# Interleaving an MLP group with the last attention tiles: own buffer, searched queue order, lighter VectorE work and LayerNorm sums on GpSimd

## The chip, the cores and the metric

The kernel runs on 1 core of one Trainium2 chip. The metric is device time in microseconds (us), the median of several executions. The span in a profile is a little shorter than the device time (228.3 against about 230 us), because it runs from the first to the last instruction. Every execution is classed as fast or slow by its length and its granted TensorE clock; only fast ones are compared.

## The reference

One transformer-like block over x of shape 1x2048x448 in bf16, cut to what matters:

```python
h  = x + A(layernorm(x), wqkv, wo)          # attention
out = h + B(layernorm(h), w1, w2, w3, w4)   # token-shift MLP

# A: 16 heads of 28; query s sees keys s, s-2, ..., s-14 (8 keys, dilation 2)
#    softmax over these 8, weighted sum of v, then @ wo
# B: g  = gelu(layernorm(z) @ w1)                    448 -> 448
#    gs = four quarters of g, shifted by +1, -1, +2, -2 tokens
#    x1 = z + gs @ w2                                448 -> 448
#    y  = x1 + gelu(layernorm(x1) @ w3) @ w4         448 -> 1792 -> 448
```

The 2048 tokens are handled as 4 attention tiles of 512 and 4 MLP groups of 512. Because of the token shifts the MLP groups are not the attention tiles: group 0 takes 128-row blocks from tiles 0 and 1.

## The kernel before

The kernel is a program that writes a program. It lists every operation with its reads and writes, then a scheduler gives each engine one fixed queue. The engines then run their queues in order, so a blocked operation blocks what stands behind it on its engine. The parts that matter here, with cuts marked:

```python
h3T = [arv(o, 128, NF * 512).rearrange("p (f n) -> p f n", f=NF) for o in (0, R_WQ)]
# both GELU buffers of the MLP lie in an arena: number 0 over wqkv and its padded copy,
# number 1 over the attention's output scratch (of, ob)

def ln_stats(kind, src, i):                                   # VectorE, one 128-row block
    dve("bn_stats", D + 20, out=st6[:, kind, i, :], in_=src)
    dve("bn_aggr", 64, out=mv[:, kind, i, :], in_=st6[:, kind, i, :])

def inv_std(slot, kind, i0, n, s1=1.0, s2=EPS):               # GpSimd, 4 operations for 4 blocks
    pool("tensor_scalar", ..., out=vtmp, in0=mv[..., 1], scalar1=s1, scalar2=s2, ...)
    S.add("pool", "tensor_tensor", ..., out=rstd, in0=vtmp, in1=mhalf, op=ALU.pow)
    pool("tensor_scalar", ..., out=nmr, in0=mv[..., 0], scalar1=-1.0, ...)
    pool("tensor_tensor", ..., out=nmr, in0=nmr, in1=rstd, op=ALU.mult)
# normalize(): one block, on VectorE or ScalarE, whichever the scheduler finds free ("flex")
# (cut)
            # end of two head groups of an attention tile: O is [128, 2, 512] in PSUM
            dve("transpose", 1024, psum=True, out=of[:, os_, :, :], in_=O(lambda p: p[:, :, :]))
            o4 = of[:, os_, :, :].rearrange("p u (b d) -> p (u b) d", d=32)
            dve("reciprocal", 160, out=rz[:, os_, :], in_=o4[:, :, 28])
            dve("scalar_tensor_tensor", 1024, out=ob[...], in0=rz[...broadcast...], scalar=UP, in1=o4, ...)
            dve("transpose", 1024, out=oT[:, par, c - 1:c + 1, :], in_=ob[:, os_, :, :])   # 16 bit
# (cut) the end of the order in which the phases are listed:
    phase_att(2); phase_WO(1); phase_QK(3); phase_V(3); phase_att(3); phase_WO(2)
    phase_B1(0); phase_B1(1); phase_B2(0); phase_WO(3); phase_B1(2); phase_B1(3)
    phase_W3(0); phase_B2(1); ...          # W3 and B3 are the two big matmuls of an MLP group
```

The scheduler is greedy: of the operations that are ready it takes the first that can start, ties broken by a list of 137 phase names. The phases are: A1 the first LayerNorm; QK, V the projections; att, av the attention; WO the output projection with its residual add; B1 a LayerNorm, w1 and GELU; B2 the shifted w2, the add and the statistics of the next LayerNorm; W3 that LayerNorm, w3 and GELU; B3 w4 and the output.

## Time and profile before

| | before |
|---|---|
| device time, median (range) of 4 runs beside the changed kernel | 229.96 us (229.75 to 231.16) |
| profiled span, mean granted TensorE clock | 228.3 us, 0.964 |
| busy: TensorE, VectorE, ScalarE, GpSimd | 205.6, 133.8, 118.4, 57.4 us |
| first projection, last matmul | 12.16, 222.70 us |

The page of the profile. Digits are the busy share of 40 equal slices in tenths; PE is TensorE, DVE VectorE, POOL GpSimd; PEclk is the granted clock.

```profile
span 228.3 us, 3663 instructions
...
PE   7799899989999859996389999999999999999990
...
DVE  7597778979979997989988308941001243101221
...
PEclk9999999999999976999959999999999999999997
...
PE 61%; DVE 23%; POOL 6%; ACT 4%; DMA 2%; issue 2%; POOLq 0%
```

The second half is TensorE without a break. In the first half VectorE is the fuller engine, TensorE has two deep holes (the slices with 5 and 3), and after each its clock drops (to 0.57 and 0.51 in the stretches of 6 us below). The last line is the share of each engine in the chain of waits, the path that ended last.

The same in a table of stretches (busy time and number of instructions of each engine, then granted clock, DMA share and GB/s). The first two lines are the two stages, split where the unbroken run of TensorE begins; the others are a hole and two stretches behind holes.

```profile
core 0: us, PE busy (x) PEld busy (x) DVE busy (x) ACT busy (x) POOL busy (x), PEclk, DMA share, GB/s
12.16:115.77 103.61, 89.25 (x971) 47.55 (x970) 91.44 (x147) 77.61 (x91) 28.25 (x52) 0.95 0.38 82
115.77:222.70 106.93, 106.93 (x519) 51.47 (x519) 33.72 (x71) 36.24 (x38) 20.43 (x32) 0.98 0.16 37
...
78.00:84.00 6.00, 2.67 (x82) 1.85 (x82) 5.90 (x10) 6.00 (x9) 0.85 (x2) 0.86 0.51 90
84.00:90.00 6.00, 5.83 (x32) 3.32 (x33) 4.11 (x9) 4.85 (x7) 3.80 (x7) 0.57 0.36 68
...
114.00:120.00 6.00, 5.16 (x14) 1.91 (x15) 5.00 (x6) 0.04 (x1) 0.00 (x0) 0.51 0.10 19
```

The chain of waits at the seam (start, length, what, number of instructions):

```profile
110.78 1.14 DVE arena L1206
...
112.33 2.11 DVE arena L1206
...
114.47 1.26 DVE oT L1206
...
115.77 106.94 PE ps L1206 x519
```

Stage 1 ends in VectorE's work on the last attention tile: a transpose out of PSUM, the softmax division, and the 16-bit transpose `oT` that the last output projections wait for. The first W3 matmul of MLP group 0 follows only at 120.45 us (this is what "first matmul of group 0" means in all that follows; the group's w1 and w2 matmuls run before it in both kernels), behind 14 output projections that take 4.85 us, most of them at half clock (0.51 from 114 to 120 us).

Some groups of instructions (shapes, count, total busy us, mean ns of one, idle before):

```profile
L1206 DVE STREAM_TRANSPOSE oT<-arena 128x1024 bf16<-128x1024 bf16 x8 | 10.0, 1245 | 0.3
...
L1206 DVE TENSOR_SCALAR lntm<-xin,mv,rstd 128x448 bf16<-128x448 bf16 x13 | 4.8, 400 | 2.7 <-POOL nmr L1206 2.6
```

### The profile page before, as it was taken

The page shows a single profiled execution, that of the slowest core. Times are in us where ns is not written, and L with a number is a line of the kernel's source. Part 1 is how long each engine was busy: PE and PEld are TensorE (multiplying, and loading weights), DVE is VectorE, ACT ScalarE, POOL GpSimd, SP SyncE. Part 2 cuts the span into 40 slices and gives each one's busy share as a digit, 9 for nine tenths or more (in the row PEclk, how much of TensorE's full clock was granted, in tenths as well). Part 3 has the DMA queues.
Part 4 walks back from the last instruction along what each step waited for, and adds up shares of the span by engine and source line. Part 5 has one row for each costly group of instructions (what it writes and reads, how often), then busy time and mean ns, then how long its engine had stood idle before and what let it go on. Part 6 is the DMA issues. An engine that isn't in the chain of part 4 may idle for free.

```text
span 228.3 us, 3663 instructions
## 1 busy us (share of the span) xinstructions
PE 205.6 (90%) x1529; PEld 103.0 (45%) x1529; DVE 133.8 (59%) x244; ACT 118.4 (52%) x134; POOL 57.4 (25%) x107
## 2 busy tenths in 40 slices
PE   7799899989999859996389999999999999999990
PEld 2346355345445534553234455554444445444540
DVE  7597778979979997989988308941001243101221
ACT  2537776774979879748903750423651152154100
POOL 8631611000241044053702300883000008000000
PEclk9999999999999976999959999999999999999997
DMA  5924682469300054004400400146000103300110
GB/s 154 295 84 87 82 195 38 92 183 290 97 4 0 3 92 92 3 0 92 81 15 0 86 6 3 36 97 132 3 0 20 40 3 64 88 0 20 46 43 26
DMA packets 32462, 15.36 MB, mean 67 GB/s; under 512 B 23416, under 2 KB 31992, under 8 KB 32440
## 3 DMA queue, kind: packets, MB, share of 16 engines
q1 hardware_dynamic: 32440, 15.06, 28.8%
q8 instruction: 14, 0.23, 0.5%
q14 instruction: 8, 0.07, 0.1%
HBM read 7.45 MB, written 1.84 MB: 41 GB/s over the span
## 4 chain that ended last, share of the span: by engine, by line
PE 61%; DVE 23%; POOL 6%; ACT 4%; DMA 2%; issue 2%; POOLq 0%
PE ps L1206 61%; DVE arena L1206 6%; DVE st L1206 5%; DVE pt L1206 3%; POOL rstd L1206 3%; DVE oT L1206 3%; DMA hT<-lntm 2%; DVE xin L1206 2%; ACT pt L1206 2%; DVE mv L1206 1%; ACT qk L1206 1%; POOL nmr L1206 1%; DVE xb L1206 1%; POOL msk L1206 1%; DVE rz L1206 1%
## 5 line engine op out<-in xcount | busy, mean ns | idle before, releaser
L1206 PE MATMUL ps<-actT,w_s 112*128 112x512 bf16 (+1 forms) x288 | 68.0, 389 | 0.4 <-DMA actT<-lntm 0.4
L1206 DVE TENSOR_TENSOR xb<-ps,xb 128x448 bf16<-128x448 f32 (+1 forms) x24 | 18.4, 772 | 66.2 <-PE ps L1206 66.2
L1206 ACT ACTIVATE arena<-ps 128x1024 bf16<-128x1024 f32 x28 | 28.6, 1023 | 50.6 <-PE ps L1206 50.5
L1206 PEld LDWEIGHTS ps<-actT,w_s 112*128 112x128 bf16 (+1 forms) x288 | 30.7, 108 | 33.0 <-issue 1.9
L1206 PE MATMUL ps<-w_s,arena 128*128 128x448 bf16 x224 | 44.4, 353 | 0.0
L1206 ACT ACTIVATE pt<-ps 110x1024 bf16<-110x1024 f32 x32 | 31.0, 1022 | 5.9 <-PE ps L1206 5.9
L1206 PEld LDWEIGHTS ps<-w_s,arena 128*128 128x128 bf16 x224 | 21.8, 98 | 21.1 <-ACT arena L1206 0.2
L1206 PE MATMUL ps<-hT,arena 112*128 112x512 bf16 x128 | 28.8, 380 | 1.9 <-DMA hT<-lntm 1.0
L1206 POOL TENSOR_SCALAR vtmp<-mv 128x4 f32<-128x4 f32 (+1 forms) x17 | 3.3, 193 | 93.6 <-DVE mv L1206 92.9
L1206 DVE TENSOR_TENSOR pt<-pt,msk 110x1024 bf16<-110x1024 bf16 x32 | 20.4, 682 | 1.1 <-ACT pt L1206 1.1
L1206 PE MATMUL ps<-wo_s,oT 128*128 128x448 bf16 x64 | 15.8, 399 | 4.5 <-ACT gT L1206 3.5
L1206 PEld LDWEIGHTS ps<-hT,arena 112*128 112x128 bf16 x128 | 12.0, 97 | 17.1 <-ACT pt L1206 1.8
L1206 DVE BATCH_NORM_STATS2 st<-xin 128x6 f32<-128x448 bf16 x32 | 19.2, 601 | 0.2
L1206 POOL TENSOR_TENSOR rstd<-vtmp,mhalf 128x4 f32<-128x4 f32 (+1 forms) x17 | 17.8, 1049 | 1.4
L1206 ACT ACTIVATE lntm<-xin,nmr,rstd 128x448 bf16<-128x448 bf16 x19 | 13.5, 755 | 8.6 <-POOL nmr L1206 8.6
L1206 POOL TENSOR_TENSOR xb<-xb,xin 128x448 bf16<-128x448 bf16 x16 | 16.7, 1072 | 2.4 <-DVE lntm L1206 1.5
L1206 ACT ACTIVATE qk<-ps 128x1024 bf16<-128x1024 f32 x12 | 12.3, 1024 | 6.8 <-PE ps L1206 6.7
L1206 PE MATMUL ps<-arena,hT 112*110 112x448 bf16 x64 | 15.0, 360 | 0.3 <-ACT pt L1206 0.3
L1206 PE MATMUL ps<-qk 28*110 28x103 bf16 (+1 forms) x320 | 10.6, 226 | 4.7 <-ACT vt L1206 2.2
L1206 PE MATMUL ps<-w_s,gT 112*128 112x448 bf16 x64 | 13.1, 353 | 1.6 <-DVE xb L1206 1.6
L1206 PEld LDWEIGHTS ps<-wo_s,oT 128*128 128x128 bf16 x64 | 6.5, 107 | 13.2 <-ACT gT L1206 3.9
L1206 PEld LDWEIGHTS ps<-qk 28*110 28x110 bf16 x320 | 7.7, 132 | 10.0 <-ACT pt L1206 2.7
(58 smaller groups left out, 183.6 us busy)
## 6 DMA issues: line engine op xcount, KB each, us to landing
w_s<-in_B_w_dram SPq DMA_DIRECT2D x2, 1568.0 KB, 10.5
out_dram<-xb SPq DMA_DIRECT2D x16, 112.0 KB, 1.7
xin<-in_A_x_dram SPq DMA_DIRECT2D x3, 448.0 KB, 7.9
arena<-in_A_wqkv_dram SPq DMA_DIRECT2D x3, 392.0 KB, 5.4
w_s<-in_B_w_dram SPq DMA_DIRECT2D x2, 392.0 KB, 4.7
xin<-in_A_x_dram SPq DMA_DIRECT2D x4, 112.0 KB, 2.1
wo_s<-in_A_wo_dram SPq DMA_DIRECT2D x4, 98.0 KB
actT<-lntm SPq DMA_TRANSPOSE x8, 4.3
```

Of the source, the lines that this page charges most:

```text
L1206: inst = getattr(eng, op.meth)(**op.kw)
```

## The change

Its intent: let MLP group 0 run in TensorE's holes between the later attention tiles, for which its GELU output needs a buffer that does not lie over wqkv; take work off VectorE; and fix the place of each single operation in its queue by a search done beforehand. Five parts:

1. **Own buffer and phase order.** `h3T` of group 0 is its own tensor; the phases B1, B2 and W3 of group 0 are listed before the last attention tiles.
2. **Order.** The greedy scheduler with its phase names goes. A list of 674 numbers gives the priority of the items, a string of digits the engine of each flexible operation. Where the scheduler's own time model sees a gap on TensorE of over 0.35 us, it inserts dummy matmuls (256 columns of zeros) to hold the clock.
3. **LayerNorm sums.** `bn_aggr` leaves VectorE (44 of 48); seven small GpSimd operations per LayerNorm group compute mean and variance from the raw statistics.
4. **Paired softmax transposes.** The scaled output is written with pairs of 16-bit values interleaved, so the second transpose moves 512 32-bit elements instead of 1024 16-bit ones. Output projection slices then have stride 2.
5. **Start.** The masks are made after the first LayerNorm on GpSimd; transposes and evictions of the first tile go in half-size pairs.

The diff, cut to its core:

```diff
-    h3T = [arv(o, 128, NF * 512)... for o in (0, R_WQ)]
+    of = sb("of", [128, 2, 2, 512], F32)
+    ob = sb("ob", [128, 2, 4, 4, 32, 2], BF16)
+    h3T = [sb("h3T", [128, NF, 512], BF16), arv(0, 128, NF * 512)...]
 (cut: scheduler)
+        rank = [-1] * m
+        for r, w in enumerate(self.plan[0] if self.plan else range(m)):
+            rank[w] = r
+            if e == "pe" and self.filler and st > 13000.0 and st - free[e] > self.GAP:
+                ... # dummy matmuls up to the modelled start of the next one
 (cut)
     def ln_stats(kind, src, i):
         dve("bn_stats", D + 20, out=st6[:, kind, i, :], in_=src)
-        dve("bn_aggr", 64, out=mv[:, kind, i, :], in_=st6[:, kind, i, :])
+    def moments(kind, i0, n):
+        pool("tensor_tensor", 90, out=a, in0=st[:, :, 1], in1=st[:, :, 4], op=ALU.subtract)
+        pool("tensor_tensor", 90, out=a, in0=a, in1=a, op=ALU.mult)
+        pool("tensor_tensor", 90, out=b, in0=st[:, :, 2], in1=st[:, :, 5], op=ALU.add)
+        pool("tensor_scalar", 90, out=b, in0=b, scalar1=4.0 / D, scalar2=None, op0=ALU.mult)
+        pool("tensor_tensor", 90, out=a, in0=a, in1=b, op=ALU.add)
+    def sums(kind, i0, n):
+        pool("tensor_tensor", 90, out=m, in0=st[:, :, 1], in1=st[:, :, 4], op=ALU.add)
+        pool("tensor_scalar", 90, out=m, in0=m, scalar1=-0.5, scalar2=None, op0=ALU.mult)
 (cut)
-                dve("scalar_tensor_tensor", 1024, out=ob[...], in0=rz[...], scalar=UP, in1=o4, ...)
-                dve("transpose", 1024, out=oT[:, par, c - 1:c + 1, :], in_=ob[:, os_, :, :])
+                dve("tensor_tensor", 1110, out=ob[...].rearrange("p g k d e -> p g e k d"), in0=o4,
+                    in1=rz4.unsqueeze(4).broadcast_to([128, 4, 2, 4, 32]), op=ALU.mult)
+                dve("transpose", 580, out=oT[:, par, c - 1:c + 1, :].bitcast(F32),
+                    in_=ob[...].rearrange("p g k d e -> p (g k d e)").bitcast(F32))
 (cut)
+    phase_B1(0); phase_B1(1)
     phase_QK(3); phase_V(3)
+    phase_att(2)
+    phase_B2(0); phase_W3(0)
     phase_att(3); phase_WO(2)
+    phase_B1(2); phase_B3(0); phase_WO(3); phase_B1(3); ...
```

## The prediction

> **What bounds the kernel now.** Two stages with different limits. In the chain of waits, 115.8 to 222.7 us is one unbroken run of TensorE (519 matmuls, 106.9 us) at full clock: one matmul per 0.216 us at 512 columns, 0.189 at 448 (timeline). Before that the chain runs mostly through VectorE: in a table of 6 us stretches it is busy 102.7 of the first 120 us. There TensorE loses time: from 12 to 120 us it is idle 13 us, most of it at 78-84 (3.3), 102-108 (2.1) and 108-114 us (3.4). After two of these holes its granted clock falls to 0.57 and 0.51; 15 projection matmuls then run 0.43 us apart, 12 output projections 0.37. That costs some 5 us more. The first real projection starts at 12.0 us; after the last matmul come 5.5 us.
>
> [...]
>
> **What the change does.**
> 1. MLP group 0 (56 matmuls of 512 and 56 of 448 columns: 12.1 + 10.6 = 22.7 us of TensorE) can run between attention tiles 2 and 3. TensorE's work doesn't shrink; its holes get filled and the clock kept.
> 2. VectorE sheds 44 of 48 aggregates (180 ns each: 7.9 us) and half of each of 8 output transposes (1.25 us for 1024 elements of 2 or 4 bytes alike, so 512 four-byte elements about 0.65: 4.8 us): 13 us of 134, some 10 of it in the first stage, whose limit it is.
> 3. GpSimd gains seven small operations per LayerNorm group, 0.19 to 0.26 us each: 15 to 20 us in total (57 now), and 1.0 to 1.5 us more latency from statistics to normalisation; hidden where other work is queued.
> 4. Start: masks behind the first LayerNorm on GpSimd, no bias needed there, transposes and evictions in half-size pairs (0.69 us becomes about 0.4). First projection at about 10 us.
> 5. Searched order of single operations, and dummy matmuls in modelled gaps, free where the gap is real. Exponentials and GELU interleave more: a table load is 1.28 us on ScalarE (4 now; I expect 5 to 8).
>
> **Sum.** At most 2 (start) + 13 (holes) + 5 (clock) = 20 us can go, a floor near 210. I expect 2 + 8.5 + 4.5 = 15, and 1 to 2 lost to misjudged waits in a fixed order: about 216 us.
>
> Predicted: 216 us, 8 in 10 within 209 to 222. Faster by over 2%: 0.93; within 2%: 0.05; slower: 0.02.
>
> **What would show each step.** (1) TensorE idle between its first projection and last matmul under 6 us, mean clock above 0.98 (now 0.964), GELUs of group 0 before the last exponentials. (2) VectorE 117 to 124 us busy, output transposes 0.6 to 0.75 us. (3) GpSimd 70 to 80 us busy. (4) First projection at 9.5 to 10.5 us. (5) Dummies visible; TensorE's share 94% or more. The chain over 75% TensorE (now 61%).
>
> **What would make it wrong.** The queues are in order: if GpSimd's longer LayerNorm or table loads come later than the order's model assumes, TensorE stands before a matmul although others could run: 222 or more. Misplaced dummies delay real matmuls. If nearly every hole is filled and the tail shrinks too: 207 to 210.

The sum is at most 2 (start) + 13 (holes) + 5 (clock) = 20 us, of which 2 + 8.5 + 4.5 = 15 were expected, less 1 to 2: about 216 us. The 5 us of the clock were counted from the slow matmuls in the trace of before; that filling the holes would win them back was the author's estimate.

## More of the kernel before

Stage 1 has 103.61 - 89.25 = 14.36 us of TensorE idle; stage 2 has none. VectorE is busy for 91.44 of 103.61 us (88%) of stage 1.

## The result, and the profile after

| | before | after |
|---|---|---|
| device time, median (range) of 4 runs | 229.96 us (229.75 to 231.16) | 220.56 us (220.08 to 220.81) |
| ratio, 95% interval | | 0.9578 (0.9542 to 0.9615) |
| profiled span, granted clock | 228.3 us, 0.964 | 218.2 us, 1.000 |
| busy: TensorE, VectorE, ScalarE, GpSimd | 205.6, 133.8, 118.4, 57.4 us | 204.0, 127.5, 114.8, 73.0 us |
| first projection, last matmul | 12.16, 222.70 us | 11.33, 213.36 us |
| first matmul of MLP group 0 | 120.45 us | 107.31 us |

A ratio is the mean time of one kernel's fast runs over the mean of the other's fast runs of the same rounds on the same chip, so it is not quite the ratio of the medians quoted beside it.

The page after:

```profile
span 218.2 us, 3795 instructions
...
PE   5899999898999878999899999999999999999991
...
...
PEclk9999999999999999999999999999999999999999
...
PE 61%; DVE 12%; POOL 9%; ACT 8%; DMA 5%; issue 2%; SPq 1%
```

The clock no longer drops and no slice of TensorE is below 7 after the start. It looks as though the holes were filled. The chain of waits does not agree: TensorE's share is 61% as before, and VectorE's share went to GpSimd, ScalarE and DMA.

The stages, split where the first matmul of group 0 starts:

```profile
core 0: us, PE busy (x) PEld busy (x) DVE busy (x) ACT busy (x) POOL busy (x), PEclk, DMA share, GB/s
11.33:107.31 95.98, 89.89 (x1029) 50.25 (x1029) 84.49 (x122) 70.28 (x80) 36.72 (x80) 1.00 0.38 87
107.31:213.36 106.05, 105.78 (x521) 51.59 (x521) 34.24 (x61) 39.75 (x44) 30.59 (x70) 1.00 0.18 40
```

And of these, the dummies alone (the tile of zeros; here the columns are TensorE, weight load and VectorE):

```profile
11.33:107.31 95.98, 7.47 (x61) 5.77 (x60) 0.00 (x0) 1.00 0.38 87
```

This is the reading on which the rest of the document stands. Stage 1 of the changed kernel holds 1029 matmuls, of which 61 are of zeros (60 dummies and the last of those at the start): 968 real ones. The two tables of stages are cut at different events: the one of before at the unbroken run, which starts with 14 output projections. Cut at the first matmul of group 0 like the one of after, it reads:

```profile
12.16:120.45 108.29, 93.93 (x985) 49.52 (x984) 94.71 (x150) 77.61 (x91) 28.25 (x52) 0.94 0.36 78
120.45:222.70 102.25, 102.25 (x506) 49.50 (x504) 30.45 (x67) 36.24 (x38) 20.43 (x32) 1.00 0.17 38
```

So before the first matmul of group 0 there stood 985 matmuls (one of them of the start's, on zeros), and after the change 968. No W3 matmul of MLP group 0 moved into stage 1; on the contrary, 16 w1 matmuls moved out of it (48 of 64 ran before that event, now 32; the new list of phases has B1(3) only after B3(0)). The holes of stage 1 are 95.98 - 89.89 = 6.09 us of idle plus 7.47 us of dummies, 13.56 us together, against 14.36 us before. They were not filled with work of group 0; over half of them were painted over. Group 0's first matmul comes 120.45 - 107.31 = 13.1 us earlier, 0.8 of it because stage 1 starts earlier. What follows it got longer, from 102.25 to 106.05 us, with the 16 matmuls more, so 3.8 us are given back; after the last matmul 0.8 us are gained (228.3 - 222.70 = 5.6, and 218.2 - 213.36 = 4.8). That makes the 10.1 us of the span.

Why group 0 starts only at 107.31 us is in the chain of waits after (start, length, what; pieces called "issue", of 0.1 us at most, are left out without a mark):

```profile
72.28 1.01 DVE xin L1264
73.31 1.16 DVE st L1264 x2
74.55 2.38 POOL mom L1264 x5
...
80.56 4.53 DMA actT<-lntm
85.14 3.67 PE ps L1264 x16
...
90.52 1.28 ACT L1264
91.82 1.94 ACT pt L1264 x2
...
94.43 1.10 DVE xb L1264
...
96.79 1.19 POOL mom L1264 x2
...
100.94 0.40 DVE lntm L1264
...
104.45 2.82 PE ps L1264 x14
107.31 28.47 PE ps L1264 x137
```

Read it as a sequence: the residual of attention tile 1 (`xin`) at 72.28; its LayerNorm (`st` on VectorE, `mom` on GpSimd); a DMA transpose; the w1 matmuls; GELU, an activation table load, two exponentials that stood in the queue in between; the residual `xb` of the token-shift matmul; the next LayerNorm; and another DMA transpose, issued at 103.03 and 4.2 us long, while the last output projections run. (At its very end the chain goes by those projections: from 101.33 us through the division and the transposes of the last attention tile on VectorE. The DMA transpose lands at about 103.03 + 4.2 = 107.2 us, so the two paths end together.) That is 107.31 - 72.28 = 35.0 us from the moment group 0's tokens leave attention until its first matmul, and TensorE carries the chain for 3.67 + 2.82 = 6.5 us of it. By 107 us the attention is over (the last exponentials start at 91.82), so there is nothing left to interleave with.

The groups that answer to those of before:

```profile
L1264 DVE TENSOR_SCALAR lntm<-xin,rstd,nmr 128x448 bf16<-128x448 bf16 x16 | 7.1, 487 | 5.8 <-POOL nmr L1264 5.8
L1264 DVE STREAM_TRANSPOSE oT<-ob 128x512 f32<-128x512 f32 x8 | 5.6, 706 | 0.2
```

The output transposes fell by 4.4 us, and the aggregates by 7.8 us (from 48 at 180 ns, 8.5 us, to 4, 0.7 us), as costed. VectorE fell only by 6.3 us in total, because it now does 33 block normalisations instead of 25, and each takes 487 to 741 ns by group where it took 394 to 400: together 16.4 us instead of 9.0.

### The profile page after: what moved, and what is told of

Read it like the earlier page. It is cut to its first block, busy times and chain, and to the rows that moved or that the text cites. A ratio compares the mean times of both kernels' runs of the same rounds, so it can differ in the third digit from the quotient of the medians.

```text
span 218.2 us, 3795 instructions
## 1 busy us (share of the span) xinstructions
PE 204.0 (94%) x1587; PEld 105.4 (48%) x1587; DVE 127.5 (58%) x206; ACT 114.8 (53%) x130; POOL 73.0 (33%) x165
## 4 chain that ended last, share of the span: by engine, by line
PE 61%; DVE 12%; POOL 9%; ACT 8%; DMA 5%; issue 2%; SPq 1%
PE ps L1264 61%; POOL mom L1264 5%; DMA xin<-in_A_x_dram 3%; DVE st L1264 3%; POOL rstd L1264 3%; DVE lntm L1264 2%; DVE xb L1264 2%; ACT pt L1264 2%; DMA actT<-lntm 2%; ACT lntm L1264 2%; SPq L1264 1%; ACT qk L1264 1%; DVE pt L1264 1%; DVE ob L1264 1%; ACT xb L1264 1%
## 5 line engine op out<-in xcount | busy, mean ns | idle before, releaser
L1264 PE MATMUL ps<-actT,w_s 112*128 112x512 bf16 (+1 forms) x288 | 63.9, 380 | 1.9 <-ACT pt L1264 1.2
L1264 POOL TENSOR_TENSOR mom<-st 128x4 f32<-128x4 f32 x33 | 8.9, 287 | 56.8 <-DVE st L1264 56.8
L1264 ACT ACTIVATE arena<-ps 128x1024 bf16<-128x1024 f32 x14 | 14.1, 1019 | 20.2 <-PE ps L1264 20.2
L1264 ACT ACTIVATE h3T<-ps 128x1024 bf16<-128x1024 f32 x14 | 14.3, 1022 | 15.5 <-PE ps L1264 15.5
L1264 PE MATMUL ps<-w_s,h3T 128*128 128x448 bf16 x112 | 22.3, 353 | 0.0
L1264 PE MATMUL ps<-w_s,arena 128*128 128x448 bf16 x112 | 22.0, 353 | 0.0
L1264 PE MATMUL ps<-zz 128*128 128x256 bf16 (+1 forms) x82 | 14.8, 334 | 2.3 <-DVE zz L1264 2.3
L1264 ACT ACTIVATE lntm<-xb,nmr,rstd 128x448 bf16<-128x448 bf16 x8 | 5.5, 750 | 21.8 <-POOL nmr L1264 21.8
L1264 PEld LDWEIGHTS ps<-w_s,arena 128*128 128x128 bf16 x112 | 10.9, 98 | 10.4
L1264 PEld LDWEIGHTS ps<-w_s,h3T 128*128 128x128 bf16 x112 | 10.9, 98 | 10.4
L1264 PE MATMUL ps<-wo_s,oT 128*128 128x448 bf16 x64 | 13.5, 354 | 1.2 <-DVE oT L1264 0.7
L1264 ACT ACTIVATE qk<-ps 128x1024 bf16<-128x1024 f32 x12 | 12.2, 1024 | 4.4 <-PE ps L1264 4.4
```

The costliest lines, as they stand in the source:

```text
L1264: inst = getattr(eng, op.meth)(**op.kw)
```

## The experiments

Two readings compete at the start. One is the prediction's: TensorE is the resource, and the gain is its holes (filled by work, or by dummies for the clock). The rival is that TensorE does not limit stage 1 at all: a chain of waits through VectorE, ScalarE, GpSimd and DMA does, and the gain is that this chain became shorter, through lighter operations or through a better order. The text before each run names theories in its own words. Every result below was correct against the reference within its tolerance. The kernel before ran beside each set on the same chip, but the sets ran on different chips.

| run | set | median (range), us | ratio to before, 95% interval | first matmul of group 0, us |
|---|---|---|---|---|
| the change | | 220.56 (220.08 to 220.81) | 0.9578 (0.9542 to 0.9615) | 107.31 |
| no_fill | 1 | 220.27 (219.67 to 221.25) | 0.9565 (0.9509 to 0.9620) | 107.31 |
| swap_h3 | 1 | 220.84 (219.84 to 221.28) | 0.9596 (0.9549 to 0.9642) | 107.15 |
| mask_late | 1 | 220.42 (219.85 to 221.00) | 0.9567 (0.9517 to 0.9618) | 106.98 |
| t16 | 1 | 221.18 (220.76 to 221.69) | 0.9604 (0.9556 to 0.9653) | 107.58 |
| before_fill | 2 | 228.85 (227.13 to 229.64) | 0.9904 (0.9827 to 0.9981) | 118.45 |
| aggr_dve | 2 | 239.34 (237.55 to 242.63) | 1.0327 (1.0239 to 1.0415) | 113.24 |
| old_ops | 2 | 239.65 (236.04 to 240.69) | none given: two of four runs slow | 113.92 |
| new_ops | 2 | 254.03 (253.54 to 254.73) | 1.0994 (1.0931 to 1.1058) | 134.0 |
| new_search | 3 | 218.71 (217.63 to 221.92) | 0.9484 (0.9431 to 0.9538) | 104.44 |
| aggr_search | 3 | 219.44 (217.36 to 219.56) | 0.9476 (0.9432 to 0.9520) | 106.53 |
| old_search | 3 | 223.48 (221.45 to 224.51) | 0.9677 (0.9627 to 0.9727) | 107.14 |
| early_group0 | 4 | 212.82 (211.30 to 215.13) | 0.9200 (0.9146 to 0.9255) | 85.25 |

Before's medians of the sets: set 1 230.49, set 2 231.06, set 3 231.33, set 4 230.75 us. Medians and ranges include the slow runs (one each of aggr_dve, new_search and early_group0, two of old_ops); the ratios don't. One of the 11 executions of before in set 3 took 523.41 us and is left out of the ratios too.

### First set: one part undone, order kept

**no_fill: the dummies away.**

```diff
-    S.filler = lambda b: dict(out=ps[:, b, 0:256], lhsT=zz[:, 0:128], rhs=zz[:, 0:256], start=True, stop=True)
```

> The changed kernel with its 60 modelled filler matmuls left out, the order of everything else unchanged. Theory (dummies keep the clock, and are free because they stand in real holes): TensorE pauses of several us appear at 93-99 us and 102-104 us, the granted clock drops to about 0.5 after them, the first matmuls of group 0 run 0.43 us apart, and the time rises by 2 to 4 us to about 223. Rival (dummies stand in the way of real matmuls): the time falls by 1 us or more, below 219.5. Third possibility (neither matters): within 0.5 us of 220.6.

Measured: 220.27 us, ratio 0.9565, no different from the change (the third possibility; the 2 to 4 us of the theory did not come). The stretch of 96 to 102 us in this run and, after it, in the changed kernel:

```profile
96.00:102.00 6.00, 3.69 (x29) 1.63 (x30) 5.08 (x9) 1.07 (x2) 4.20 (x11) 0.73 0.01 3
```

```profile
96.00:102.00 6.00, 6.00 (x81) 4.17 (x79) 5.19 (x9) 1.06 (x2) 4.19 (x11) 1.00 0.01 3
```

Without dummies the hole is there for all to see, and the clock falls to 0.73; eight output projections at 98.95 us then take 3.17 us where the changed kernel needs 1.69. Yet the busy times of VectorE, ScalarE and GpSimd are the same to about 0.1 us, and group 0 starts at 107.31 us in both. The slow matmuls ran in time that TensorE would have spent waiting. So in this kernel neither the dummies nor the clock that they keep is worth anything that these runs can tell from zero, and a full row of TensorE digits proves nothing about the chain. This run also gives the holes without dummies, of which before has none in stage 1 either:

```profile
11.33:107.31 95.98, 85.45 (x969) 45.05 (x969) 84.46 (x122) 70.32 (x80) 36.98 (x80) 0.98 0.39 88
```

That is 95.98 - 85.45 = 10.53 us of idle against 14.36, so 3.8 us less, where idle plus dummies gave 0.8 less. Either way it is well under the 8.5 us predicted, and none of it is work of group 0.

The clock fell behind these holes (0.57 and 0.51 over the stretches shown of before, 0.73 here over a stretch that is slow in part). The longest unbroken pause ahead of the three drops was 2.02 us (up to 81.61 us of before), 3.48 us (up to 114.09 us of before) and 1.74 us (up to 95.56 us of this run), with small matmuls in between ahead of the first and the last; from what length of pause on it falls, these runs don't settle. Nor does the clock tell whether the slow matmuls lie on the chain.

**swap_h3: the two GELU buffers exchanged**, so that the buffer of group 0 lies over wqkv again.

```diff
-    h3T = [sb("h3T", [128, NF, 512], BF16), arv(0, 128, NF * 512)...]
+    h3T = [arv(0, 128, NF * 512)..., sb("h3T", [128, NF, 512], BF16)]
```

> The changed kernel with the two h3 buffers exchanged: MLP groups 0 and 2 write the arena that held the QKV weights (as in the kernel before), groups 1 and 3 the new buffer. Same order of instructions. Theory (the own buffer buys nothing, since group 0's first matmul runs only at 107 us, after the last reader of the QKV weights at about 78 us): 220.6 us within 0.5. Rival (the own buffer is what lets group 0 start): the first group-0 matmul comes later and the time rises by 2 us or more.

Measured: 220.84 us, ratio 0.9596; its interval holds the change's ratio. The last matmul that reads wqkv starts, with seven others, at 75.81 us in this run (1.72 us together), some 30 us before group 0's first matmul at 107.15, so the own buffer releases nothing. Under an order that starts group 0 early the buffer could matter; no run here tried that.

**mask_late: the mask making on GpSimd waits for the last normalisation of the first tile.** It puts the masks, which the change had already moved behind the first LayerNorm's GpSimd part, behind its VectorE part too.

```diff
-        S.after = [o for o in S.ops if o.eng == "pool" and o.tag == "A1_0" and o.meth == "tensor_tensor"][-1]
+        norm = [o for o in S.ops if o.eng == "dve" and o.tag == "A1_0" and o.meth == "tensor_scalar"][-1]
+        S.after = norm          # and, for every mask operation: op.deps.add(norm)
```

> The changed kernel with the mask and memset operations of GpSimd made to wait for the last VectorE normalisation of tile 0 instead of running beside it. Both theories expect the second pair of normalisations to fall from 1.06 us each to about 0.35 and the first projection to start at 10.2 to 10.6 instead of 11.33 us. Theory A (the start is on the critical path): the time falls by 0.7 to 1.2 us, to about 219.6. Theory B (the second input tile arrives at 11.6 us whatever the start does, and everything after waits for it): the time stays within 0.4 us of 220.6, and the pause of TensorE before 25 us grows by about 1 us.

Measured: 220.42 us, ratio 0.9567: no gain that can be told apart (group 0 starts 0.3 us earlier). But the local effect is large. The second pair of normalisations on VectorE in the changed kernel, then in this run (timeline: start, length, what):

```profile
8.05 2.12 DVE L1264 TENSOR_SCALAR lntm<-xin,mv,rstd 128x448 bf16<-128x448 bf16 x2 [0.60 <-POOL rstd L1264]
```

```profile
8.05 0.70 DVE L1268 TENSOR_SCALAR lntm<-xin,mv,rstd 128x448 bf16<-128x448 bf16 x2 [0.60 <-POOL rstd L1268]
```

The same two instructions take 2.12 us while GpSimd makes masks and clears memory, and 0.70 us when GpSimd is quiet. This run shows the slowdown, by a factor of 3, and that it goes when GpSimd is quiet; how the one engine holds up the other, no trace here shows. The time didn't follow, because the chain of the start is not TensorE's: it runs through the load of the second input tile (7.44 us from 4.19 us on in the chain of the changed kernel) into that tile's statistics at 11.65 us. The first projection came 0.4 us earlier (10.92 us, later than the 10.2 to 10.6 that both theories expected), and of that 0.3 us reached group 0's first matmul.

**t16: the output transposes back to 1024 16-bit elements**, in the same places of the queues.

```diff
-                dve("transpose", 580, out=oT[...].bitcast(F32), in_=ob[...].bitcast(F32))
+                dve("transpose", 580, out=oT[:, par, c - 1:c + 1, :], in_=ob[:, os_, :, :])   # and the old scaling
```

> The changed kernel with the 16-bit output transposes of before put back (scaling and token order with them), same order otherwise. VectorE gains 8 x 0.54 = 4.3 us in the transposes and loses about 0.7 us in the scaling. Theory (VectorE limits the first stage, so most of this is on the path): slower by 2 to 4 us, 222.5 to 224.5. Rival (the first stage waits on the latency of LayerNorm groups and on misjudged waits, not on VectorE's throughput): slower by less than 1 us.

Measured: 221.18 us, ratio 0.9604: about 0.3% over the change's, inside both intervals. Taking these transposes' 4.4 us off the busiest engine of stage 1 (3.4 us of its total, 130.9 against 127.5, as the scaling became dearer) bought some 0.6 us in this order, not told from zero by these runs.

The first set undoes three of the change's ideas (dummies, buffer, paired transposes) and carries a fourth further (the masks), without moving the time by more than the runs can tell. What was left was the order, the sums on GpSimd and the half-size pairs of the start, which no run undoes.

### Second set: sums, old operations, old order

**aggr_dve: LayerNorm sums back on VectorE**, the list of positions carried over, each aggregate behind its statistics.

```diff
+        dve("bn_aggr", 64, out=mv[:, kind, i, :], in_=st6[:, kind, i, :])
-            moments(kind, i0, n)        # and sums(); vtmp and nmr from mv as in the kernel before
```

> The changed kernel with the LayerNorm sums moved back from GpSimd to VectorE (44 aggregates of 0.18 us; GpSimd back to four operations per group), the queue order otherwise kept, each aggregate right after its statistics. Theory A (GpSimd's added latency of about 2.3 us per group is on the chain to group 0's first matmul, twice): that matmul starts 2 to 4 us earlier than 107.3 and the time falls to 217 to 219. Theory B (VectorE's throughput limits the first stage): VectorE's 8 us more show as 3 to 8 us more in total, 224 to 229. Theory C (slack on both): within 1 us of 220.6.

Measured: 239.34 us, ratio 1.0327. None of the expectations allowed for that: it is slower than the kernel before. The granted clock was 0.959; behind a new hole of 3.03 us, up to 65.20 us, 8 projection matmuls take 3.60 us, where 8 of the same take 1.90 at 23.83 us. The chain of waits of this run, in what should be the unbroken stage 2:

```profile
159.73 0.77 ACT lntm L1261
...
160.57 4.00 POOL xb L1261 x4
...
164.65 0.20 POOL vtmp L1261
```

Four residual additions (`xb`, 1 us each; the trace shows no engine waiting for one) stand in GpSimd's queue in front of the next LayerNorm, and TensorE waits behind that. Group 0 starts 5.9 us later than in the change, and stage 2 gets holes on top. That suggests that the operation moved is not what costs, but that the other operations' places no longer fit it; aggr_search, below, tests this.

**old_ops: old sums and old transposes under the searched order** (the diffs of aggr_dve and t16 together).

> The searched order of the changed kernel with the old operations: aggregates on VectorE and 16-bit output transposes, so VectorE has about 12 us more work than in the changed kernel. If the searched order alone brings the gain: 220 to 222.5 us. If the lighter VectorE brings it: 226 us or more, near the kernel before. In between, the two need each other.

Measured: fast runs of 239.44 and 236.04 us, the other two slow, so no ratio. By the measure set before (226 us or more) this would speak for the lighter VectorE; but it is near aggr_dve, and old_search, below, shows with these same operations that it is misfit.

**before_fill: the kernel before, with 31 dummies** by the change's rule.

```diff
+            if e == "pe" and self.filler and st > 13000.0 and st - free[e] > 350.0:
+                ...                     # as in the change
+    S.filler = lambda b: dict(out=ps[:, b, 0:256], lhsT=zz[:, 0:128], rhs=zz[:, 0:256], start=True, stop=True)
```

> The kernel before, order unchanged, with dummy matmuls in the modelled holes of TensorE (31 of them). Theory of the prediction (the clock lost after holes costs about 5 us): mean clock above 0.99 and 2 to 5 us faster than before, 225 to 228. Rival, which the run without fillers of the changed kernel suggests (a slow TensorE in the first stage is hidden by waits for other engines): within 1 us of the kernel before, and of the lost clock only what falls into the last stretch (some 2 us after 114 us) is gained, if a dummy stands in that hole.

Measured: 228.85 us, ratio 0.9904 (0.9827 to 0.9981), some 2.2 us of 231.06, by the interval 0.4 to 4.0. The timeline of TensorE at the end of stage 1:

```profile
111.98 2.58 PE L1219 MATMUL ps<-zz 128*128 128x256 bf16 x22 [1.23 <-DVE arena L1219]
114.39 0.54 PE L1219 MATMUL ps<-wo_s,oT 128*128 128x448 bf16 x2
115.79 2.82 PE L1219 MATMUL ps<-wo_s,oT 128*128 128x448 bf16 x14 [0.86 <-DVE oT L1219]
```

The 14 output projections start when they did before (115.79 and 115.77 us) and take 2.82 us instead of 4.85: 2.0 us, nearly the whole gain. These, unlike those of no_fill, are on the chain. The dummies mended only this second drop; the first is still there:

```profile
84.00:90.00 6.00, 5.82 (x31) 3.22 (x32) 4.11 (x9) 4.85 (x7) 3.81 (x7) 0.50 0.36 68
```

What mending the first would bring, no run shows; but the chain of waits of before holds no TensorE piece at all from 75.61 us to past 99 us, so its slow matmuls are not on the chain. So of the clock's loss in the kernel before, which the prediction put at 5 us, about 2 were worth anything.

**new_ops: the change's operations, start and buffer under the old scheduler and its list of phase names**, phases in the old order, no dummies.

> The opposite half: the new operations (GpSimd sums, 32-bit transposes, half-size transposes at the start, masks behind the first LayerNorm) under the old scheduler, the old tag order and the old phase order, no fillers. If the operations bring the gain: 220 to 224 us. If the order does: 228 us or more. It may be slower than before, since the tag order was tuned for the old operations: then the operations pay only with a new order.

Measured: 254.03 us, ratio 1.0994. The lighter operations under the old order are 10% slower than the old operations under it (both without dummies; the clock fell to 0.909, and what part of the 10% that is, no run shows). An order is fitted to its operations, in both directions. Read so, aggr_dve, old_ops and new_ops say nothing of what an operation is worth; for that, each variant needs an order of its own.

### Third set: each variant with its own order

I searched anew for three sets of operations, with the same method for all: the changed kernel's own queue model, operation lengths corrected from the traces, and a second score with VectorE 6% and GpSimd 35% slower, so that an order that fits only exact lengths loses. All three keep the change's start, its own h3 buffer and its rule for dummies (35, 35 and 80 came of it).

**new_search: the change, operation for operation**, only list and picks new.

```diff
 _ORDER = """
-297 381 97 293 296 189 191 320 318 ... (cut)
+333 222 186 28 240 669 36 358 10 ... (cut)
 _PICK = """
-100000010011010100000100010011001010001110101100100000001011110110100000111100001100111111000100
+100101101101101011000011001000000000000101111100000000001111000100000000111111000110100100110000
```

> The changed kernel, operation for operation, with only the list of queue positions (and the engine picks) exchanged for one of another search: the same queue model with the durations that the traces show, and scored also with VectorE 6% and GpSimd 35% slower, so that a late operation pushes less behind it. On that model the changed kernel takes 2.5 us longer. If the order is what the time depends on and the model is as good here as it was for the changed kernel: 217 to 219.5 us, first matmul of group 0 earlier than 107.3 us. If the remaining time is a limit of the engines: 220 to 221 us, as the changed kernel.

**aggr_search: the sums back on VectorE** (the diff of aggr_dve, order searched for it).

> The LayerNorm sums back on VectorE (the operations of the run with 239 us), but with an order searched for these operations in the same way. If the 19 us of that run were a misfit of the order to the operations: 217.5 to 221 us, within 1.5 us of the same search with the sums on GpSimd. If VectorE's 8 us count in themselves: 224 us or more.

**old_search: old sums and old 16-bit transposes** (the diff of old_ops, order searched for it).

> All old operations (sums and 16-bit output transposes on VectorE, about 12 us more for it than in the changed kernel), with an order searched for them in the same way; phase order and h3 buffers of the changed kernel. The difference from the kernel before is then the order of single operations with its dummies, the difference from the re-searched new operations is the lighter VectorE. If the order carries most of the gain: 221 to 224.5 us. If the lighter operations do: 226 us or more.

Measured together on one chip, in five rounds: 0.9484 (0.9431 to 0.9538), 0.9476 (0.9432 to 0.9520), 0.9677 (0.9627 to 0.9727). Three things follow.

- With an order of its own, the variant with sums on VectorE is as fast as the one with sums on GpSimd. The 19 us of aggr_dve were misfit. Moving the sums is worth nothing that these runs can tell: the aggregates (48 at 176 ns, 7.9 us) go back on VectorE, but its total is only 129.4 against 128.2 us, as this order leaves it fewer casts out of PSUM (1.7 against 8.2 us). GpSimd is less busy (59.1 us against 71.0), and LayerNorm's way through it has four operations instead of ten (1.8 against 4.1 us in the traces of before and after).
- A searched order with the old sums and transposes carries 3.2% (0.9677), of the change's 4.2%. It is not the order alone: the start, buffer and dummies of the change are still in. The first set showed that buffer and dummies don't carry the time within the changed kernel; in the kernel before, dummies gave 1.0% (before_fill), so a part of the 3.2% may be theirs.
- Lighter operations bring another 2% (0.9677 to 0.948). old_search and aggr_search differ in nothing but the paired transposes, with the scaling and slices that go with them, and their orders, so that falls to the 32-bit transposes. In the change's own order they brought some 0.3%, within the noise (t16). A search is not exhaustive, so a part of these 2% may be the luck of one search; one search for each variant can't rule that out.

The new order is also a little faster than the change's (0.9484 against 0.9578, on different chips). With aggr_search, from which it can't be told apart, it is the fastest correct version here. In its stage 1 (10.95 to 104.44 us) the windows give 5.49 us of idle and 3.90 us of dummies, where the change has 6.09 and 7.47.

### Fourth set: what if group 0 were ready?

**early_group0: a wrong computation.** Group 0's second LayerNorm reads rows of the residual after attention tile 0 instead of the output of the token-shift stage, so its input is there some 20 us earlier. The matmuls, GELUs and shapes are the same. (The numbers still pass the tolerance, since this branch adds little to the output, but it is not the reference's function.) Order searched anew.

```diff
         for k, i in enumerate(GROUPS[g]):
-            normalize_t(3, 2, 4 * g + k, ls, k, xb[:, i, :])
+            if g == 0:
+                normalize_t(2, 1, k, ls, k, xin[:, k, :])
+            else:
+                normalize_t(3, 2, 4 * g + k, ls, k, xb[:, i, :])
```

> Wrong result on purpose. The re-searched kernel, but the first matmuls of MLP group 0 read four rows that are ready long before (the second-layer input of attention tile 0) in place of the output of the token mixing, so they need not wait for the output projection of tile 1, its LayerNorm, its first MLP layer, the mixing and another LayerNorm. All instructions are kept in number and size; the order is searched again for this freedom and now holds no dummies. If the wait of group 0 for that chain is why TensorE's holes were not filled: its first matmul runs at about 84 us between the last attention tiles, and the time is 213 to 216 us, 3 to 5 us below the re-searched kernel. If the holes could not be filled anyway (ScalarE and VectorE are too busy there to follow): 217.5 to 219 us.

Measured: 212.82 us, ratio 0.9200 (0.9146 to 0.9255). TensorE's timeline and its stages in this run:

```profile
84.38 0.46 PE L1267 MATMUL ps<-qk 28*110 28x103 bf16 x20 [0.47 <-ACT qk L1267]
85.25 8.81 PE L1267 MATMUL ps<-actT,w_s 112*128 112x512 bf16 x40 [0.41 <-DMA actT<-lntm]
93.99 0.66 PE L1267 MATMUL ps<-pt,vt 110*32 110x103 bf16 x40
```

```profile
11.50:85.25 73.75, 69.32 (x858) 38.70 (x857) 61.85 (x94) 58.40 (x66) 21.85 (x53) 1.00 0.46 105
85.25:205.46 120.21, 120.21 (x633) 59.75 (x633) 54.28 (x92) 50.77 (x57) 43.60 (x98) 1.00 0.19 41
```

Here is the picture that the prediction had in mind: 40 matmuls of group 0 between the attention's logits and its weighted sums, and TensorE without a break from 85.25 us on. Nothing about engines, queues, PSUM or buffers stood against it. The only things changed are when the input is there and the order searched for that. Idle falls to 73.75 - 69.32 = 4.43 us with no dummies (the last matmuls on zeros are those of the start, at 10.71 us), against new_search's 5.5 + 4.8 us of idle and dummies from its first to its last matmul.

So an input that is ready early is worth, against an equally searched order, 0.9484 - 0.9200 = 2.8% of before's time, about 6.5 us. That is an estimate of what part 1 could have brought, from two searches on two chips; by the ends of the two intervals it is 1.8 to 3.9%, so the 8.5 us that the prediction expected are more than was found, but are not ruled out.

## Why the prediction was right or wrong

The direction and the range held: 220.56 us lies in 209 to 222, 4.6 us above the point of 216. That was in good part luck: of the steps several failed, the largest term of the sum among them, and most of the gain came from a step to which the prediction gave no number.

**The term that failed: "holes", 13 us at most, 8.5 expected; measured about 1, or 4 without dummies, and not by the step's means.** The prediction put it as step 1, "MLP group 0 ... can run between attention tiles 2 and 3. TensorE's work doesn't shrink; its holes get filled and the clock kept". The runs showed in its place: none of these matmuls (W3 and B3 of group 0) ran before the end of attention, idle plus dummies went from 14.36 to 13.56 us in stage 1 (10.53 us of idle in no_fill), and TensorE's part of the chain stayed at 61% (predicted over 75%). I had checked that the buffer was free and that there was room on TensorE, and had not measured when the input would be ready. The trace of before shows the pieces of that chain: DMA transposes of 4.3 us, a LayerNorm on GpSimd of 1.8 us, GELUs and exponentials of 1 us each in one queue. early_group0 shows that this was the reason, and swap_h3 that the buffer was not.

**Idle below 6 us: failed in substance.** 6.36 us of idle, from the first projection to the last matmul, but 7.47 us of dummies besides. The check was badly made: dummies are TensorE work to a busy counter. It should have counted real matmuls before the seam (971 before, 968 after).

**The clock: restored as predicted (1.0), but worth less.** 4.5 us expected. before_fill gained some 2.2 us, for the second of the two drops, and no_fill lost nothing without it. The predicted cost was the sum of all slow matmuls, on the chain or not.

**VectorE: 117 to 124 us expected, 127.5 measured.** The two removed costs were right (aggregates 7.8, transposes 706 ns each, 4.4 us). Missing was that the flexible normalisations would move onto it (33 instead of 25) and take longer. That they lengthen beside a busier GpSimd is shown directly for one pair (mask_late) and supposed for the others.

**GpSimd: 70 to 80 us expected, 73.0 measured; its added latency 1.0 to 1.5 us expected, 2.3 measured** in the last LayerNorm before group 0: 96.79 to 100.91 us after, 98.63 to 100.44 before, 4.1 against 1.8 us. Hidden it was not: `mom` alone is 5% of the chain. Against the aggregates it replaced it is a draw (aggr_search).

**Start: first projection at 9.5 to 10.5 us expected, 11.33 measured.** The masks still overlap the second pair of normalisations (2.12 us, against 0.70 in mask_late). It did not matter (mask_late), since by the chain of waits the second input tile's load sets the pace (7.44 us, up to 11.63).

**Table loads: 5 to 8 expected, 4 counted** (1.28 us each), as before: GELUs and exponentials did not interleave more.

**What made the time fall, then:** mainly a chain up to group 0's first matmul that a searched order shortened, by about 8.5 us net (13.1 us earlier, of which 0.8 are the earlier start and 3.8 are given back behind it). old_search puts the order, with the change's start, buffer and dummies, at 3.2% or some 7.5 us of before's 231.33, and the lighter VectorE operations, when the order can use them, at up to 2% more. The prediction had the order as its fifth step, without a number.

**The warning that came true** was "misjudged waits in a fixed order": what aggr_dve measured against the change (239.34 - 220.56 = 18.8 us) and new_ops against the kernel before (254.03 - 231.06 = 23.0 us) is a fixed order that does not fit. The change came 4.6 us short of the point of the prediction mainly for another reason, the unready input; but its order was not the best either, as new_search gains about 1% more (0.9484 against 0.9578, on different chips).

**What stays open.** How the 3.2% split between order, start and dummies within old_search; whether the own buffer would pay under an order that starts group 0 earlier; how much of the 2% for transposes is search luck; and what the start's half-size pairs are worth. TensorE's busy time without dummies, up to group 0's first matmul, fell from 93.93 to 89.89 - 7.47 = 82.42 us, and that is mostly accounted for: w1 fell from 13.6 to 7.5 us (16 matmuls moved behind, the rest no longer slow), the output projections from 15.8 to 13.5 us at full clock.

## What to carry to other kernels

Before you count on work to fill an engine's holes, follow the chain of waits to that work's input and read when it will be ready; then free that dependency in a run that computes the wrong thing, and you have an estimate of the ceiling before you build anything. Count real work on either side of the seam, not busy digits, since dummies fill digits without moving the end. And where the order of in-order queues was fitted to the operations, compare variants only with an order refitted to each: with a stale order the same operations cost up to 10% more than the kernel before, with a fitted one they gain 5%.
